# Moving the size pass of expert 1's first matrix into the attention's tail, its rows ahead of two raw pieces, and the later raw pieces and all converted pieces onto GpSimd's queue

## The chip, the cores and the metric

One core of a Trainium2 chip runs the whole program. Its engines, as the profile names them: PE (matmul; PEld is its weight load), DVE, ACT, POOL, and SP, which computes nothing and issues DMAs. A row "SPq" or "POOLq" is an issue of a DMA by that engine. The metric is the device time of one execution in microseconds; the median of three runs is compared.

## The reference, cut to what matters

Three layers in a row. First an attention with a decay (softmax-free), 4 batches of 576 tokens, 8 heads of 64. Then a mixture of 8 experts: each token goes to one expert `e`, found by a gate and a running rule along the sequence, and becomes `p[e] * (max(x @ w1[e], 0) @ w2[e])` with `w1[e]` 512x1024 and `w2[e]` 1024x512. Last a Fourier mixing with a layer norm and a two-matrix channel block whose weights `w_ch1` and `w_ch2` are 64-bit floats in the input.

```python
h = np.maximum(x[b, s] @ w1[e], 0.0)
out[b, s] = p[e] * (h @ w2[e])
...
ch = np.maximum(un @ w_ch1, 0.0) @ w_ch2
```

The kernel reads `w_ch1` and `w_ch2` as pairs of 32-bit integers and builds 32-bit floats from them.

## The kernel before, in words

**Order of the work.** `attention` runs 18 steps and routes tokens into rows of `xs` in DRAM, sorted by expert. Its tail (the calls after the loop, lines 760 to 800) already computes the hidden layer of the 256 tokens of expert 0's second part (`hidden`, line 692). Then `moe` runs: two output tiles of that part (line 1111), then the loop over experts `e = 0..7` (line 1119). Expert `e` has eight hidden blocks `f` (12 matmuls each of `n` columns: weights high times tokens high, low times high, high times low), then one output tile per 128 tokens (24 matmuls of 512 columns each). `n` is 128 for expert 0 in this loop and 416 for the first of the sorted experts, which the text calls expert 1; 320 or 288 for the next ones.

**Preparing a matrix.** A matrix comes as four pieces of 128x1024 floats (512 KB each, `Weights.load`, issued by SP, tile `wst`). Each needs its size: an ACT pass of absolute values with a running sum (`absmax`, line 234), which writes its useless output into the target `wh`. From the four sums DVE makes a small diagonal (`peak`, line 243, last operation line 255), PE spreads it over the partitions (`spread`, line 260), DVE makes the scale (`scale`, lines 266 and 269), and each piece is then split (`split`): ACT writes the high half (line 276), DVE the low half (line 281).

**A hidden block's exit.** `relu` (line 816): ACT writes the high half (823), DVE the low half (825). Hidden blocks rotate through four PSUM banks, so block 4 of an expert waits until DVE has read block 0.

**Converting.** 14 jobs (`Doubles`) turn a raw 1 MB piece of `w_ch1` or `w_ch2` into a 512 KB piece in DRAM (`ch`), in the shadow of the experts. A job is `load` (SP, tile `raw`, two buffers), `first` (DVE, lines 294, 296, 298), `second` (DVE, lines 303, 306), `absmax` (ACT, tile `ab`) and `store` (SP, line 338). `halves` (line 924) lists by hand at which block or tile each of these and each step of the next matrices is issued.

**Tokens.** `fetch(e)` (line 1005) reads the rows of expert `e` by a transposing DMA into `xt` (line 1012) and then their metadata `mt` with one to five small DMAs (lines 1025, 1028). `pad(e)` (line 1040) writes zeros into `xs` ahead; a later `fetch` waits for it.

**Every queue runs in order.** An engine's instruction that waits holds back all behind it. SP issues all of the loads above, so a raw load that waits for its buffer holds back the next weights and tokens. All SP transfers are on one hardware queue; the indirect stores of POOL (line 851) are on another, made by software. Line 402 puts the scratch row of the routing into expert 1's low half (`spare[1]`), so `beyond` (line 2063), its last reader, must come before the first split.

Of the kernel before, what the change touches and what calls it, by code (L numbers as in the profile page):

```python
# [9 lines left out]
FP32 = mybir.dt.float32  # L10
# [10 lines left out]
E, FF = 8, 2048  # L21
# [17 lines left out]
CAP = max(CAPS)  # L39
# [170 lines left out]
class Weights:  # L210
# [9 lines left out]
    def load(self, j):  # L220
        t = self.pool.tile([128, 1024], FP32, tag="wst", name="wst")
        src = self.src[j]
        to = t.rearrange("p (a d) -> p a d", a=2) if len(src.shape) == 3 else t
        self.nc.sync.dma_start(out=to, in_=src)
        self.pieces[j] = t
# [85 lines left out]
class Doubles:  # L311
# [4 lines left out]
        self.nc, self.pool, self.jobs, self.raw, self.t = nc, pool, jobs, {}, {}  # L316

    def load(self, j):
        r = self.pool.tile([128, 1024, 2], I32, tag="raw", name="raw", bufs=2)
        src = self.jobs[j][0]  # L320
        to = r.rearrange("p (a d) c -> p a d c", a=2) if len(src.shape) == 4 else r
        self.nc.sync.dma_start(out=to, in_=src)
        self.raw[j] = r

    def first(self, j):
# [9 lines left out]
        w.size(i, self.t[j].bitcast(FP32), x)  # L335

    def store(self, j):
        self.nc.sync.dma_start(out=self.jobs[j][1], in_=self.t[j].bitcast(FP32))


def attention(keep, tc, nc, A, xs, rows, hook, beside, after, zeros, first, spare, hid0, mt0):

    ctx = ExitStack()
    cp = ctx.enter_context(tc.tile_pool(name="const", bufs=1))
# [57 lines left out]

    carry = keep.tile([128, 17], BF16, name="carry")
    V.memset(carry, 0.0)
    room = spare[1][0:1, 0, :].bitcast(FP32)
    n_i, pick, tally, who, low, start, beyond = order(nc, A, keep, room, carry, onesb)
    slot_i = const("slot_i", [128, N], I32)
    slot_f = const("slot_f", [128, N])
# [381 lines left out]
    next(early[4])  # L790
    first.low(6)
    first.low(7)
    next(early[5])
    next(early[6])
    next(early[7])
# [4 lines left out]
    return idn, n_i, who, low, start, beyond  # L800


def products(nc, ps, h, l, xt, f):

    for i, (m, x) in enumerate(((h, 0), (l, 0), (h, 4))):
        for k in range(4):
            nc.tensor.matmul(  # L807
                out=ps,
                lhsT=m[:, k, 128 * f : 128 * f + 128],
                rhs=xt[:, x + k, :],  # L810
                start=(k == 0 and i == 0),
                stop=(k == 3 and i == 2),
            )


# [48 lines left out]
class Late:  # L864


    def __init__(self, nc, w, pool, x2, rows):
        self.nc, self.w, self.pool, self.x2, self.rows = nc, w, pool, x2, rows
        self.n, self.hid = CAPS[E - 1] - HEAD, None

    def hidden(self, fs, bank):

# [104 lines left out]
def moe(octx, tc, nc, A, xs, x2, rows_in, rows_out, pieces, weights, who, conv, low, start, beyond, z, hid0, mt0, wst, small):  # L977
# [6 lines left out]
    p2 = pool(name="p2", bufs=3, space=PSUM)  # L984
    weights(0).shared.bank = lambda: p2.tile([128, 512], FP32, tag="ps2", name="peak")[:, 0:128]
    X = {}
    end = Late(nc, weights(E - 1), wst, x2, rows_out)

    side = {}
    for k in (2, 4):  # L990
# [14 lines left out]
    def fetch(e):  # L1005
        n = CAPS[e] if e < E - 1 else HEAD
        xt = wk.tile([128, 8, n], FP16, tag="xt", name="xt", padded_shape=[128, 8, CAP])
        at = lambda a, m: slice(OFF + a, OFF + a + m) if e == 0 else bass.ds(low(e) + a, m)
        for j in range(2) if e == 0 else (None,):

            a, b = (0, 2) if j is None else (j, j + 1)
            i = nc.sync.dma_start_transpose(out=xt[:, 4 * a : 4 * b, :], in_=xs[at(0, n), 512 * a : 512 * b])
            if e == 0:
                rows_in.before(i)
            apart(e, i)
        if e == E - 1:
# [12 lines left out]
        if e == E - 1:  # L1029
            k = (n + 127) // 128  # L1030
            i = nc.sync.dma_start(
                out=mt[:, k : k + m // 128, :], in_=meta(n, m // 128 * 128).rearrange("(t p) c -> p t c", p=128)
            )
            apart(e, i)
            more = m % 128
            for j in range(0, 128, more) if more else ():
                apart(e, nc.sync.dma_start(out=mt[j : j + more, k + m // 128, :], in_=meta(n + m // 128 * 128, more)))
        X[e] = (xt, mt)

    def pad(e):  # L1040
        m = CAPS[e] - ZERO
        i = nc.sync.dma_start(
            out=xs[bass.ds(start(e), m), :].bitcast(I32).rearrange("(t p) c -> p t c", p=32),
            in_=z[0:32].bitcast(I32).unsqueeze(1).to_broadcast([32, m // 32, XW // 2]),
        )
        apart(e, i)

    def factors(w, mt, tiles):

        q = wk if w is not end.w else small  # L1050
        fs = q.tile([128, 5], FP32, tag="fs", name="fs", bufs=3)

        def fill():
            nc.vector.tensor_tensor(out=fs[:, 4:5], in0=w.inv[:, 0:1], in1=w.inv[:, 1:2], op=ALU.mult)
            nc.vector.tensor_scalar(
                out=fs[:, 0:tiles], in0=mt[:, 0:tiles, 1].bitcast(FP32), scalar1=fs[:, 4:5], scalar2=None, op0=ALU.mult
            )

        return fs, fill
# [15 lines left out]
        w1.load(p)  # L1075
    fetch(0)
    pad(1)
    conv.load(0)
    conv.load(1)
    fetch(1)  # L1080

    def begin():
        for p in range(4):
            w1.absmax(p)
        w1.peak(0)

    def parts():
        beyond()
        w1.spread(0)
        w1.scale(0)  # L1090
        w1.split(0)
        w1.split(1)

    def convert(n):
        conv.first(n)
        conv.second(n)
        conv.store(n)
        conv.load(n + 2)

    def sizes():  # L1100
        for p in range(4, 8):
            w1.absmax(p)
        convert(0)
        w1.peak(1)
        conv.absmax(0)
        convert(1)

    fs, fill = factors(weights(0), mt0, 2)
    fill()
    for t in range(2):  # L1110
        out(weights(0), hid0, mt0, fs, t, n, [(begin, parts)[t]])

    v = weights(2)
    first = [[] for _ in range(8)]
    for f, p in ((1, 2), (3, 3)):
        first[f].append(partial(w1.split, p))
    for f, p in zip((2, 3, 4, 5), range(4)):
        first[f].append(partial(v.load, p))
    for e in range(E):
        w, n = weights(e), CAPS[e] if e < E - 1 else HEAD  # L1120
        if e == E - 1:
            pieces.more = None
        xt, mt = X.pop(e)
        tiles = (n + 127) // 128

        todo = halves(weights, conv, 2 * e, 8, [("fetch", (fetch, e + 1))] if e + 1 < E else ()) if e else first
        hid = wk.tile([128, 2, 8, n], FP16, tag="hid", name="hid", padded_shape=[128, 2, 8, CAP])
        hid = [hid[:, x] for x in range(2)]
        for f in range(8):
            ps = p1.tile([128, CAP], FP32, tag="ps1", name="ps1")[:, 0:n]  # L1130
            products(nc, ps, *w.dst, xt, f)
            for do in todo[f]:
                do()
            if f == 4 and e + 2 < E:
                pad(e + 2)
            for _ in relu(nc, ps, hid, f):
                pass
        fs, fill = factors(w, mt, tiles + (end.n + 127) // 128 if e == E - 1 else tiles)
        if e == E - 1:
            end.fs = fs  # L1140

        def sides(mt=mt, tiles=tiles, n=n, e=e):
            for i, m in ((n // 128, n % 128), (tiles + end.n // 128, end.n % 128 if e == E - 1 else 0)):
                if m:

                    to, k = mt[:, i, 0:1], 128 // m
                    nc.vector.tensor_scalar(out=to, in0=to, scalar1=float(k), scalar2=side[k], op0=ALU.mult, op1=ALU.add)

        late = 0 < e < E - 1
        if not late:  # L1150
# [998 lines left out]
def fused_kernel(tc, A, out, stop=None):  # L2149
    nc = tc.nc  # L2150
    with ExitStack() as ctx:
# [5 lines left out]
        with tc.manual_schedule():  # L2157
# [101 lines left out]
                for p in range(4):  # L2259
                    weights(1, who).load(p)  # L2260

            idn, n_i, who, low, start, beyond = attention(keep, tc, nc, A, xs, rows_in, hook, beside, after, z, weights(0), bufs[1], hid0, mt0)
            fill.close()
            tp = ctx.enter_context(tc.tile_pool(name="tp", bufs=1, reuse_waits="tile"))
            tables = []
# [62 lines left out]
```

## Time and profile before

| | us |
|---|---|
| median of 3 runs | 802.59 (800.28 to 808.28) |
| the profiled execution | 806.81, its span 805.0 |
| PE busy in the span | 738.7 (92%) |
| DVE, ACT, POOL busy | 591.2, 411.8, 130.0 |

The rows below come from the profiled execution. Times in a timeline are counted from the span's start. The expert stage runs from about 130 to 349 us; the Fourier and channel stage follows. A busy PE is not a PE at its peak, and matmul ends are modelled. PEclk is the granted clock of PE as a share of 2.4 GHz; 0.5 is its other level, 1.2 GHz.

### The profile page before, as it was taken

The numbers are of one execution on the slowest core, as the hardware profiler recorded it, in microseconds if no ns is written. First come the engines' busy times: TensorE is split into PE (matmuls) and PEld (weight loads), VectorE is DVE, ScalarE is ACT, GpSimd is POOL, SyncE is SP. The second block draws the span as 40 slices with busy tenths as digits, with TensorE's granted clock in tenths as the row PEclk, the third lists the DMA queues.
The fourth block names the chain that finished last, engine by engine and source line by source line (L and its number), as shares of the span: only waits on it lengthen the run. The fifth ranks groups of instructions, "written<-read, shape, count | busy, mean of one in ns | idle before, by whom it ended". The sixth has DMA issues, their size and how long they took to land. (4 is left out here: it accounts for less than half of the span.)

```text
span 805.0 us, 17230 instructions
## 1 busy us (share of the span) xinstructions
PE 738.7 (92%) x6571; PEld 552.4 (69%) x6571; DVE 591.2 (73%) x1432; ACT 411.8 (51%) x829; POOL 130.0 (16%) x225
## 2 busy tenths in 40 slices
PE   7889898898999998889989998979899999999996
PEld 5778774644666555557634546868788888888885
DVE  3577886887889887957697986968968495737362
ACT  1355655676978797844836534515523361404140
POOL 3555443103012201113000011010010101010101
PEclk9999999999999999999999999999999999999998
DMA  8997439999999998961447357620370016210000
GB/s 288 354 295 270 163 107 275 244 330 339 289 379 281 270 362 292 265 217 42 130 130 273 132 173 193 181 66 2 104 207 2 27 53 171 53 39 16 27 2 27
DMA packets 91930, 142.29 MB, mean 177 GB/s; under 512 B 48116, under 2 KB 49017, under 8 KB 90814
## 3 DMA queue, kind: packets, MB, share of 16 engines
q1 hardware_dynamic: 87246, 126.78, 50.7%
q0 software_dynamic: 4592, 14.31, 4.7%
q8 instruction: 54, 0.88, 0.5%
q14 instruction: 38, 0.31, 0.1%
HBM read 97.55 MB, written 35.12 MB: 165 GB/s over the span
## 5 line engine op out<-in xcount | busy, mean ns | idle before, releaser
L1628 PE MATMUL g<-gxt,wh 128*128 128x256 f16 (+1 forms) x992 | 142.9, 284 | 4.6 <-DMA gxt<-un 3.4
L1942 PEld LDWEIGHTS <-hd 128*128 128x128 f16 x1176 | 115.1, 98 | 28.0 <-issue 7.7
L1628 PEld LDWEIGHTS <-wh 128*128 128x128 f16 x1056 | 103.0, 98 | 30.0 <-issue 8.3
L281 DVE SCALAR_TENSOR_TENSOR wl<-wst,ws,wh 128x1024 f16<-128x1024 f32 (+1 forms) x82 | 100.6, 1252 | 11.3 <-ACT wh L276 11.1
L276 ACT ACTIVATE wh<-wst,ws 128x1024 f16<-128x1024 f32 x80 | 89.4, 1141 | 28.7 <-DVE ws L269 28.3
L807 PE MATMUL ps<-xt,wh 128*128 128x320 f16 (+4 forms) x544 | 80.0, 285 | 12.1 <-DMA xt<-xs 7.5
L837 PE MATMUL ps<-wh,hid 128*128 128x512 f16 (+2 forms) x528 | 84.6, 302 | 0.2 <-ACT hid L823 0.2
L807 PEld LDWEIGHTS <-wh 128*128 128x128 f16 x640 | 58.6, 101 | 37.5 <-issue 16.0
L1942 PE MATMUL g<-wh,hd 128*128 128x256 f16 x448 | 79.9, 276 | 4.2 <-DVE u L1971 2.0
L1802 POOL DMA_INDIRECT out<-u,orow x18 | 19.3, 1075 | 392.0 <-DVE u L1971 293.6
L1628 PE MATMUL g<-gxt,wl 128*128 128x256 f16 (+1 forms) x496 | 79.5, 283 | 0.0
L837 PEld LDWEIGHTS <-hid 128*128 128x128 f16 (+2 forms) x792 | 46.5, 100 | 44.4 <-issue 4.7
L1913 DVE SCALAR_TENSOR_TENSOR s<-g,r 128x256 f32<-128x256 f32 x168 | 53.2, 372 | 30.6 <-ACT hd L1907 29.9
L234 ACT ACTIVATE wh<-wst 128x1024 bf16<-128x1024 f32 x66 | 69.3, 1051 | 3.8 <-DVE wst L306 3.8
L1971 DVE SCALAR_TENSOR_TENSOR u<-g,ffs,u 128x256 f32<-128x256 f32 (+1 forms) x63 | 34.2, 568 | 50.4 <-PE g L1942 48.5
L1906 ACT ACTIVATE r<-g 128x256 f32<-128x256 f32 x56 | 21.1, 377 | 91.7 <-PE g L1628 85.7
L1886 ACT ACTIVATE hd<-s 128x640 f16<-128x640 f32 x56 | 41.3, 737 | 47.1 <-DVE s L1913 47.1
L1942 PE MATMUL g<-e,hd 128*128 128x256 f16 x504 | 60.0, 273 | 5.5 <-DVE u L1971 4.5
L851 POOL DMA_INDIRECT x<-y,mt x25 | 32.3, 1291 | 197.5 <-ACT y L849 143.6
L1942 PE MATMUL g<-wl,hd 128*128 128x256 f16 x224 | 61.8, 276 | 0.0
L1628 PEld LDWEIGHTS <-wl 128*128 128x128 f16 x528 | 51.7, 98 | 11.4 <-issue 0.5
L837 PE MATMUL ps<-wl,hid 128*128 128x512 f16 (+2 forms) x264 | 56.5, 301 | 0.1
(302 smaller groups left out, 1301.0 us busy)
## 6 DMA issues: line engine op xcount, KB each, us to landing
wst<-in_moe_w SPq DMA_DIRECT2D x64, 512.0 KB
raw<-in_ch SPq DMA_DIRECT2D x14, 1024.0 KB
qk<-in_qkv SPq DMA_DIRECT2D x18, 512.0 KB
vk<-in_qkv SPq DMA_DIRECT2D x16, 512.0 KB
pair<-ch SPq DMA_DIRECT2D x32, 256.0 KB
ch<-d SPq DMA_DIRECT2D x14, 512.0 KB
wst<-ch SPq DMA_DIRECT2D x14, 512.0 KB
u<-u SPq DMA_DIRECT2D x9, 512.0 KB
```

The source lines that it names most:

```text
L234: self.nc.scalar.activation(out=x, in_=t, func=ACTF.Abs, accum_out=self.am[:, j : j + 1])
L276: self.nc.scalar.activation(out=self.dst[0][:, j, :], in_=self.pieces[j], func=ACTF.Copy, scale=self.by(j))
L281: self.nc.vector.scalar_tensor_tensor(out=l[:, j, c], in0=self.pieces[j][:, c], scalar=self.by(j), in1=h[:, j, c], op0=ALU.mult, op1=ALU.s ...
L807: nc.tensor.matmul(out=ps, lhsT=m[:, k, 128 * f : 128 * f + 128], rhs=xt[:, x + k, :], start=(k == 0 and i == 0), stop=(k == 3 and i == 2),)
L837: nc.tensor.matmul(out=ps[r * j : r * j + r, 0:d], lhsT=hid[x][:, f, 128 * t : 128 * t + r], rhs=m[:, 4 + f // 2, c : c + d], start=(f == ...
L851: nc.gpsimd.indirect_dma_start(out=x2[:, :].rearrange("t (k d) -> (t k) d", k=k), out_offset=bass.IndirectOffsetOnAxis(ap=mt, axis=0), in_ ...
L1628: nc.tensor.matmul(out=ps, lhsT=m[:, k + 4 * (f // 8), 128 * (f % 8) : 128 * (f % 8) + 128], rhs=xt[x][:, k, :], start=(k == 0 and i == 0) ...
L1886: nc.scalar.activation(out=hd[:, 0, 2:7], in_=s, func=ACTF.Copy, scale=C2 / 2)
L1906: nc.scalar.activation(out=r, in_=p[:, 1:3], func=ACTF.Relu)
L1913: V.scalar_tensor_tensor(out=d, in0=x, scalar=0.0, in1=y, op0=ALU.max, op1=op)
L1942: nc.tensor.matmul(out=ps, lhsT=hid[k][:, y, x, :], rhs=E[w][m][k], start=(k == 0 and m == y == 0), stop=(k == 7 and y == 1),)
L1971: V.scalar_tensor_tensor(out=y, in0=p, scalar=fs[:, c : c + 1], in1=y, op0=ALU.mult, op1=ALU.add)
```

## The change: what it does

Expert 1's first matrix: its four size passes leave `begin` and go into the attention's tail, ahead of the exits of hidden blocks 6 and 7 of expert 0's second part. Its spread stands inside the second output tile and no longer behind it, and all four splits follow at once. The scratch row moves to the high half of piece 6, so `beyond` moves from ahead of the scale to hidden block 7 of expert 0. The size passes of pieces 4 and 5 of expert 1 move up to block 0 of expert 0.

Expert 0's eight blocks are computed in two groups of four banks: all high-times-high products of a group, then high-times-low, then low-times-high.

SP's queue: `fetch(1)` now stands ahead of raw pieces 0 and 1. Raw pieces 2 to 13 and all 14 stores are issued by POOL. In `sizes`, `peak(1)` of expert 1 stands between `first(0)` and `second(0)`, not behind both.

```diff
     def load(self, j):
+        q = self.nc.gpsimd if j > 1 else self.nc.sync
...
-        self.nc.sync.dma_start(out=to, in_=src)
+        q.dma_start(out=to, in_=src)
...
     def store(self, j):
-        self.nc.sync.dma_start(out=self.jobs[j][1], in_=self.t[j].bitcast(FP32))
+        self.nc.gpsimd.dma_start(out=self.jobs[j][1], in_=self.t[j].bitcast(FP32))
...
-    room = spare[1][0:1, 0, :].bitcast(FP32)
+    room = spare[0][0:1, 6, :].bitcast(FP32)
...
     first.low(7)
+    sizes()
     next(early[5])
...
     fetch(0)
     pad(1)
+    fetch(1)
     conv.load(0)
     conv.load(1)
-    fetch(1)
...
     def parts():
-        beyond()
-        w1.spread(0)
         w1.scale(0)
-        w1.split(0)
-        w1.split(1)
+        for p in range(4):
+            w1.split(p)
...
     def sizes():
-        for p in range(4, 8):
-            w1.absmax(p)
-        convert(0)
+        for p in range(6, 8):
+            w1.absmax(p)
+        conv.first(0)
         w1.peak(1)
+        conv.second(0)
+        conv.store(0)
+        conv.load(2)
         conv.absmax(0)
-        convert(1)
+        conv.first(1)
+        conv.second(1)
+        conv.store(1)
+        conv.load(3)
...
-    for f, p in ((1, 2), (3, 3)):
-        first[f].append(partial(w1.split, p))
+    for p in range(4, 6):
+        first[0].append(partial(w1.absmax, p))
+    first[7].append(beyond)
...
+            if e == 0 and f % 4 == 0:
+                four = [bank()[:, 0:n] for _ in range(4)]
+                for part in (0, 2, 1):
+                    for g in range(4):
+                        products(nc, four[g], *w.dst, xt, f + g, (part,))
...
+            def sizes():
+                for p in range(4):
+                    weights(1).absmax(p)
```

**SP's queue around the tokens of expert 1.** Before, from the pad (`xs<-z`) on; `xt` are the tokens, `mt` their metadata, TENSOR_LOAD reads the row number into SP:

```order
L1042 DMA xs<-z 32x9x528
L322 DMA raw<-in_ch 128x2048 x2
L2046 TENSOR_LOAD n_i
L2046 ISA x2
L1012 ISA
L1012 DMA_TRANSPOSE xt<-xs 128x8x416
L1025 ISA
L1025 DMA mt<-xs 128x3x2
```

Now, at the same place, to the first weight piece of the matrix after expert 1's:

```order
L1050 DMA xs<-z 32x9x528
L2056 TENSOR_LOAD n_i
L2056 ISA x2
L1020 ISA
L1020 DMA_TRANSPOSE xt<-xs 128x8x416
L1033 ISA
L1033 DMA mt<-xs 128x3x2
...
L1036 DMA mt<-xs 32x2
L323 DMA raw<-in_ch 128x2048 x2
```

The two raw loads moved behind the transposing load and five metadata loads.

**DVE at the start of the conversion, just behind expert 0's hidden blocks.** Before (`d` is the converted piece, `wm` and `diag` are `peak(1)` of expert 1):

```order
L1055 TENSOR_SCALAR fs<-mt,fs 128x1
L294 TENSOR_SCALAR d<-raw 128x1024
L296 TENSOR_SCALAR d<-d 128x1024
L298 TENSOR_SCALAR d<-d 128x1024
L303 SCALAR_TENSOR_TENSOR d<-raw,d 128x1024
L306 SCALAR_TENSOR_TENSOR d<-raw,d 128x1024
L250 TENSOR_REDUCE wm<-am 128x1
L251 TENSOR_SCALAR wm<-wm 128x1
L255 TENSOR_SCALAR diag<-idn,wm 128x128
```

Now:

```order
L1062 TENSOR_SCALAR fs<-mt,fs 128x1
L294 TENSOR_SCALAR d<-raw 128x1024
L296 TENSOR_SCALAR d<-d 128x1024
L298 TENSOR_SCALAR d<-d 128x1024
L250 TENSOR_REDUCE wm<-am 128x1
L251 TENSOR_SCALAR wm<-wm 128x1
L255 TENSOR_SCALAR diag<-idn,wm 128x128
L303 SCALAR_TENSOR_TENSOR d<-raw,d 128x1024
L306 SCALAR_TENSOR_TENSOR d<-raw,d 128x1024
```

The diagonal stands two long operations earlier, still behind the first operation that needs raw piece 0; behind these rows follow, in both, the whole of job 1 and then the spread's reduction.

**POOL's queue from the two stores of expert 0's second part on.** Before, the indirect stores (`y` into `x2`) stand alone:

```order
L851 DMA x_58<-y,mt_88 2304x512
L186 MEMSET mark_x_74 1x8
L851 DMA x_58<-y,mt 2304x512
L186 MEMSET mark_x_74 1x8
```

Now:

```order
L855 DMA x_58<-y,mt_88 2304x512
L186 MEMSET mark_x_74 1x8
L339 DMA ch<-d 128x1024
L323 DMA raw<-in_ch 128x2048
L339 DMA ch<-d 128x1024
L323 DMA raw<-in_ch 128x2048
L855 DMA x_58<-y,mt 2304x512
L186 MEMSET mark_x_74 1x8
L339 DMA ch<-d 128x1024
L323 DMA raw<-in_ch 128x2048
```

Each store and each raw load from piece 2 on now stands among the indirect stores, behind the conversion that it waits for.

## Rows read from the trace of the kernel before

**Rows 1.** Stages: us, busy PE, PEld, DVE, ACT, POOL (instructions), clock, DMA share, GB/s

```profile
141.30:145.10 3.80, 3.80 (x40) 3.76 (x39) 3.52 (x5) 2.76 (x6) 1.57 (x2) 0.55 1.05 377
...
153.90:156.20 2.30, 0.06 (x2) 0.04 (x1) 2.19 (x6) 1.73 (x3) 0.00 (x0) 1.00 0.75 23
...
196.70:301.80 105.10, 102.01 (x808) 64.11 (x812) 93.02 (x157) 89.62 (x151) 15.06 (x20) 1.00 1.00 321
...
304.90:309.00 4.10, 4.10 (x21) 2.74 (x21) 2.33 (x8) 0.73 (x1) 1.34 (x3) 0.58 0.77 188
```

**Rows 2.** Waits of PE, 115 to 165 us: us in total, times, longest

```profile
PE ps L807 <- DMA xt<-xs: 4.7, 2, 2.4
```

**Rows 3.** Timeline around expert 1: start, us, engine, line, operation [idle before <- releaser]

```profile
139.35 2.95 SPq L322 DMA_DIRECT2D raw<-in_ch  x2
...
144.49 7.63 SPq L1012 DMA_TRANSPOSE xt<-xs  x1
...
149.68 0.69 DVE L294 TENSOR_SCALAR d<-raw 128x1024 int32<-128x1024 int32 x1
...
152.40 0.42 SPq L1025 DMA_DIRECT2D mt<-xs  x1
...
153.09 2.72 SPq L1028 DMA_DIRECT2D mt<-xs  x4
...
154.65 0.29 DVE L255 TENSOR_SCALAR diag<-idn,wm 128x128 bf16<-128x128 f32 x1
...
156.16 0.86 PE L807 MATMUL ps<-xt,wh 128*128 128x416 f16 x4 [2.24 <-DMA xt<-xs]
...
156.97 1.23 SPq L224 DMA_DIRECT2D wst<-in_moe_w  x3
...
158.29 1.22 DVE L306 SCALAR_TENSOR_TENSOR d<-raw,d 128x1024 int32<-128x1024 int32 x1
...
163.03 0.58 DVE L825 SCALAR_TENSOR_TENSOR hid<-ps,hid 128x416 f16<-128x416 f32 x1
...
171.25 0.69 DVE L294 TENSOR_SCALAR d<-raw 128x1024 int32<-128x1024 int32 x1 [2.03 <-DMA raw<-in_ch]
...
173.09 0.59 PE L837 MATMUL ps<-wh,hid 128*128 128x512 f16 x2
```

**Rows 4.** Waits of SP, 130 to 200 us

```profile
SPq L1012 <- DMA xs<-z: 1.1, 1, 1.1
```

**Rows 5.** Timeline of an earlier transposing load, in the attention's tail

```profile
109.55 2.69 SPq L680 DMA_TRANSPOSE wh<-xs  x2
...
113.41 0.61 PE L807 MATMUL ps<-wh,wh 128*128 128x256 f16 x4 [0.78 <-DMA wh<-xs]
```

**Rows 6.** Timeline, later waits of PE and DVE in the expert stage

```profile
177.42 0.22 PE L260 MATMUL ps<-diag,onesb 128*128 128x128 bf16 x1 [1.57 <-DVE diag L255]
...
184.09 1.67 SPq L322 DMA_DIRECT2D raw<-in_ch  x1
...
193.85 0.72 DVE L294 TENSOR_SCALAR d<-raw 128x1024 int32<-128x1024 int32 x1 [5.22 <-DMA raw<-in_ch]
...
196.71 0.23 PE L260 MATMUL peak<-diag,onesb 128*128 128x128 bf16 x1 [2.17 <-DVE diag L255]
...
304.89 0.65 PE L807 MATMUL ps<-xt,wh 128*128 128x288 f16 x4 [2.84 <-DMA xt<-xs]
```

**Rows 7.** Timeline of ACT in the attention's tail

```profile
129.93 0.38 ACT L821 ACTIVATE r<-ps 128x256 f32<-128x256 f32 x1 [4.59 <-DVE wl L281]
...
132.25 1.04 ACT L234 ACTIVATE wh<-wst 128x1024 bf16<-128x1024 f32 x1
```

**Rows 8.** POOL's mark (ns: least, median, most) and DVE beside its longest

```profile
L186 POOL MEMSET mark_x<- x25: 94/94/646, 138.3 to 380.6; 1x8 f32 x25
...
222.79 0.69 DVE L298 TENSOR_SCALAR d<-d 128x1024 int32<-128x1024 int32 x1
...
222.87 0.65 POOL L186 MEMSET mark_x<- 1x8 f32 x1
```

More of the change, by code (lines that the diff above doesn't have):

```diff
@@ L337, in store, with attention @@
     def store(self, j):
-        self.nc.sync.dma_start(out=self.jobs[j][1], in_=self.t[j].bitcast(FP32))
-def attention(keep, tc, nc, A, xs, rows, hook, beside, after, zeros, first, spare, hid0, mt0):
+        self.nc.gpsimd.dma_start(out=self.jobs[j][1], in_=self.t[j].bitcast(FP32))
+def attention(keep, tc, nc, A, xs, rows, hook, beside, after, sizes, zeros, first, spare, hid0, mt0):
     ctx = ExitStack()
@@ L800, in attention, with products @@
     return idn, n_i, who, low, start, beyond
-def products(nc, ps, h, l, xt, f):
-    for i, (m, x) in enumerate(((h, 0), (l, 0), (h, 4))):
+def products(nc, ps, h, l, xt, f, parts=range(3)):
+    last = 2 if len(parts) == 3 else 1
+    for i in parts:
+        m, x = ((h, 0), (l, 0), (h, 4))[i]
         for k in range(4):
@@ L811, in products @@
                 start=(k == 0 and i == 0),
-                stop=(k == 3 and i == 2),
+                stop=(k == 3 and i == last),
             )
@@ L867, in __init__, with w @@
     def __init__(self, nc, w, pool, x2, rows):
-        self.nc, self.w, self.pool, self.x2, self.rows = nc, w, pool, x2, rows
+        self.nc, self.of, self.pool, self.x2, self.rows = nc, w, pool, x2, rows
         self.n, self.hid = CAPS[E - 1] - HEAD, None
+    @property
+    def w(self):
+        return self.of()
     def hidden(self, fs, bank):
@@ L986, in moe @@
     X = {}
-    end = Late(nc, weights(E - 1), wst, x2, rows_out)
+    end = Late(nc, lambda: weights(E - 1), wst, x2, rows_out)
     side = {}
@@ L1046, in pad, with factors @@
         apart(e, i)
-    def factors(w, mt, tiles):
-        q = wk if w is not end.w else small
+    def factors(w, mt, tiles, q=wk):
         fs = q.tile([128, 5], FP32, tag="fs", name="fs", bufs=3)
@@ L1077, in moe, with parts @@
     pad(1)
+    fetch(1)
     conv.load(0)
     conv.load(1)
-    fetch(1)
-    def begin():
+    def parts():
+        w1.scale(0)
         for p in range(4):
+            w1.split(p)
+    def sizes():
+        for p in range(6, 8):
             w1.absmax(p)
-        w1.peak(0)
-    def parts():
-        beyond()
-        w1.spread(0)
-        w1.scale(0)
-        w1.split(0)
-        w1.split(1)
[L1094 to L1100, printed above, removed]
-        for p in range(4, 8):
-            w1.absmax(p)
-        convert(0)
+        conv.first(0)
         w1.peak(1)
+        conv.second(0)
+        conv.store(0)
+        conv.load(2)
         conv.absmax(0)
-        convert(1)
+        conv.first(1)
+        conv.second(1)
+        conv.store(1)
+        conv.load(3)
     fs, fill = factors(weights(0), mt0, 2)
     fill()
+    w1.peak(0)
     for t in range(2):
-        out(weights(0), hid0, mt0, fs, t, n, [(begin, parts)[t]])
+        out(weights(0), hid0, mt0, fs, t, n, (parts,) if t else (), partial(w1.spread, 0) if t else None)
     v = weights(2)
     first = [[] for _ in range(8)]
-    for f, p in ((1, 2), (3, 3)):
-        first[f].append(partial(w1.split, p))
+    for p in range(4, 6):
+        first[0].append(partial(w1.absmax, p))
+    first[7].append(beyond)
     for f, p in zip((2, 3, 4, 5), range(4)):
@@ L1129, in moe @@
         for f in range(8):
-            ps = p1.tile([128, CAP], FP32, tag="ps1", name="ps1")[:, 0:n]
-            products(nc, ps, *w.dst, xt, f)
+            if e == 0 and f % 4 == 0:
[3 more added lines that the diff above has]
+                        products(nc, four[g], *w.dst, xt, f + g, (part,))
+            if e == 0:
+                ps = four[f % 4]
+            else:
+                ps = bank()[:, 0:n]
+                products(nc, ps, *w.dst, xt, f)
             for do in todo[f]:
@@ L1137, in moe @@
                 pass
-        fs, fill = factors(w, mt, tiles + (end.n + 127) // 128 if e == E - 1 else tiles)
+        fs, fill = factors(w, mt, tiles + (end.n + 127) // 128, small) if e == E - 1 else factors(w, mt, tiles)
         if e == E - 1:
@@ L2260, in after, with sizes @@
                     weights(1, who).load(p)
-            idn, n_i, who, low, start, beyond = attention(keep, tc, nc, A, xs, rows_in, hook, beside, after, z, weights(0), bufs[1], hid0, mt0)
+            def sizes():
+                for p in range(4):
+                    weights(1).absmax(p)
+            idn, n_i, who, low, start, beyond = attention(keep, tc, nc, A, xs, rows_in, hook, beside, after, sizes, z, weights(0), bufs[1], hid0, mt0)
             fill.close()
```

## The prediction

> **What bounds the kernel now.** I read the stages first. In the expert stage PE is the engine that is full: from 196.7 to 301.8 us it is busy 102.01 of 105.10 us [rows 1]. So a change in this stage is worth only what it adds to or takes from the few gaps of PE, and I went on to the waits of PE and then to the timeline at each gap. Near expert 1 there are two gaps, both for tokens (`xt`): 4.7 us in total [rows 2], of which the second, 2.24 us, ends at 156.16 [rows 3]. Later there are 1.57 and 2.17 us in front of a spread, whose diagonal DVE makes late, and 2.84 us for the tokens of a later expert [rows 6]. DVE made those diagonals late because it stood in front of a raw piece: 2.03 us [rows 3] and 5.22 us [rows 6]. All gaps that this change can reach are thus 2.24 + 1.57 + 2.17 + 2.84 = 8.8 us, and what the clock adds: behind the last one the granted clock is 0.58 over 4.1 us [rows 1], the lower level for most of it, which costs 4.1 x 0.42 = 1.7 us. After the first gap it is 0.55 for 3.8 us [rows 1]; that gap stays, since `fetch(0)` and what is ahead of it in SP's queue are unchanged.
>
> **The tail of the attention.** Four size passes of 1.04 us [rows 7] move from behind ACT's last hidden exit to before the last two. ACT stands idle there for 4.59 us [rows 7], but the last pieces may land late in that gap; two exits then end up to 0.8 us later, and PE reads them in the eighth block of the tile that runs. I take 0.3 us. Bounds: 0 and the four passes, 4.2 us. Regrouping expert 0's 96 matmuls removes and adds none; it needs four banks at once, so block 4's group waits for four exits; I take 0, at most the 1 us that four exits might lag. Moving `beyond` costs DVE nothing: it stood in the way of the scale and now stands where DVE has no other work. All of this lies ahead of the new wait below and is swallowed by it, up to 3.7 us.
>
> **Tokens of expert 1 and raw pieces 0 and 1.** Before, two raw loads (2 MB) were issued at 139.35, ahead of the transposing load at 144.49 [rows 3]. That load cannot start much earlier: SP waited 1.1 us for the pad to land right before it [rows 4], and the pad stays where it is. But nothing large is ahead of it any more. An earlier transposing load of 256 rows took SP 2.69 us [rows 5]; 416 rows are 4.4 us, so SP is through at 148.9 and not at 152.1, and with the 1.2 us from the end of such an issue to PE's start [112.24 to 113.41, rows 5] the tokens are there at 150.1. PE is done with expert 0 at 156.16 - 2.24 = 153.9, with the tail's 0.3 at 154.2: the gap of 2.24 us goes.
>
> What is late next is raw piece 0. SP needs 3.7 us for the five metadata loads (from 152.12 to 155.81, rows 3) and so issues it at 148.9 + 3.7 = 152.6. It lands 0.4 us of issue (1.23 for three, rows 3) + 2.8 us of transfer (1.05 MB at 377 GB/s, rows 1) + 1.2 us later: at 157.0. The lower bound leaves out the last term, 155.8; the upper is the 9.8 us which the loaded queue took from the issue at 184.09 to the start at 193.85 [rows 6], 162.4. I take 157.0, since the DMAs moved only 23 GB/s at that place [rows 1]. DVE began this conversion at 149.68 [rows 3], so DVE is 7.3 us late.
>
> What is queued behind that wait: on DVE the diagonal, both conversions, then the scale and the exit of hidden block 0. From 149.68 to the diagonal's end at 154.94 less the two second operations (2.46 us) is 2.8 us in the new order, so PE's spread, queued behind block 0 (one block is (173.09 - 156.16) / 8 = 2.12 us, rows 3), gets it at 157.0 + 2.8 + 0.2 = 160.0: PE stands from 156.3, 3.7 us. Then PE does blocks 1 to 3, and block 4 waits for block 0's exit. Before, the conversions ended at 159.51, 9.83 us after their start, and the exit 4.1 us later at 163.61 [rows 3], 1.0 us ahead of PE's block 4 at 156.16 + 4 x 2.12 = 164.6. Now the exit ends at 157.0 + 9.83 + 4.1 = 170.9 and block 4 starts at 171.0: **PE is 6.4 us behind the old kernel**, the 2.24 us gained already counted.
>
> **Later raw pieces on POOL's queue.** Before, raw pieces 2 and 4 were asked for by SP late, behind other loads; now POOL asks as soon as DVE is through with the buffer. Raw 2 is asked for about 162.5 and needed at 171.25 - 2.03 + 7.3 = 176.5; even 9.8 us suffice. So the 2.03 us go, DVE is 5.3 us late, and the spread at 177.42 comes at 182.7, where PE (6.4 behind, but formerly waiting 1.57 us) arrives at 182.3: 5.3 us behind. Raw 4 likewise: DVE asks 5.22 us earlier, and the 2.17 us go: 3.1 us behind. I price POOL's issues themselves at nothing: POOL is busy 15.06 of 105.10 us [rows 1], its indirect stores have three output buffers, and each raw piece has a spare of over 5 us; without that cover the price is the slow rival below.
>
> POOL's mark takes 94 ns and once 646 ns, beside a DVE operation of the kind that starts each conversion [rows 8]. The Trainium skill (SBUF — State Buffer, section SBUF: two separate sides) says that while DVE runs an operation that uses both ports GpSimd is locked out and cannot write the descriptors of its own DMAs. The trace agrees for a memset; no run here shows a plain DMA on this queue. By that rule the three such operations of a conversion delay a raw load by up to 3 x 0.69 = 2.1 us, which changes the sum by nothing while the spare holds, and feeds the slow rival.
>
> The gap of 2.84 us and its clock, together 4.5 us: the tokens of that expert stood in SP's queue behind a raw piece and a store, 1.57 MB or 4.9 us at 321 GB/s [rows 1]. These now go on another queue but over the same DMA engines. Bounds 0 and 4.5 gained; nothing in the trace decides, I take 2.2. Two new waits of some 4 us may bring the low clock once more, 0 to 1.7 us (the second of them partly behind DVE's lateness); I take 0.6.
>
> **Sum:** 6.4 - 1.1 - 2.2 - 2.2 + 0.6 = +1.5 us. The profiled execution took 806.81 (span 805.0), so 808.3 by its own time; it is 4.2 us above the median of the three runs, 802.59, and by that the forecast is 804.
>
> **Rivals.** (a) *Slow: the conversions do not catch up.* If raw 2 lands after 178.5 and raw 4 later than 199, because POOL's issues are held by DVE, the waits of 2.03 and 5.22 us stay: PE keeps DVE's 7.3 us, the later gap stays, and with 1.2 us of clock it is +8.5 us, 811. For it: the 646 ns row and DVE's load of 93.02 of 105.10 us [rows 1]; against it: the spares. (b) *Fast: raw piece 0 in time.* If it lands by 148.8, block 4 finds its exit done, and the gaps go without the price: -(1.9 + 1.57 + 2.17 + 4.5) = -10.1 us, 792.5. Against it: SP itself is not free before 148.9. A landing between costs 1 us per us, and so does a later one, up to +5.4 us at 162.4. (c) *The other queue only shares the engines.* Then the gap at 304.89 stays whole: +3.7 us, 806.3. The Trainium skill (DMA: Bandwidth & Descriptors, section Queues, rings and completion order) says that each DMA engine serves its queues in turn, packet by packet. No row here shows two large transfers on two queues; by that rule the 1.57 MB still pass before the tokens, which is this rival. (d) The whole gap goes: -0.7 us, 801.9.
>
> **Chances.** A measurement of this kernel can tell about 1% (8 us) from no change. Forecast with (d) 0.55, its own range 799 to 807; (c) 0.20; (a) 0.15; (b), or a landing early enough for most of it, 0.10. Faster by over 1% needs (b): 0.10. Slower needs (a): 0.15. Within 1%: 0.75. The range takes in (a) at its edge and half the way to (b): 797 to 811.
>
> **What would show it.** Right: no wait for tokens at expert 1's start; DVE idle in front of L294 from about 150 to 157; PE idle some 3.7 us before the first spread of expert 1 and again before its block 4; no DVE wait for raw pieces after that. Wrong: raw piece 0's conversion starting before 153, or no gap at the spread (then the sum is too high by that); DVE waits for raw pieces from POOL's queue (then too low); a different length of what follows the expert stage, which I leave as it is.

## The result, and the profile after

| | before | after |
|---|---|---|
| median, executions | 803.05 us (6: 800.28 to 808.28) | 813.16 us (6: 810.96 to 829.71) |
| ratio | | 1.0129 [1.0092, 1.0166] |
| profiled execution, its span | 806.81, 805.0 | 812.88, 811.0 |

The change makes the kernel 1.3% slower; the forecast was 804 us, at most 811. The ratio leaves out executions over 1.5% above a kernel's fastest, so it is not the quotient of the medians. The executions after are also spread far more widely than those before, which is half of the story below. The profiled execution before lies 3.8 us above its median, the one after at its median, so the two traces differ by 6.1 us and the medians by 10.1.

Expert 1 went much as forecast. PE's waits after, 115 to 165 us, which answer to [rows 2]:

```profile
PE peak L260 <- DVE diag L255: 4.4, 1, 4.4
PE ps L811 <- DVE hid L829: 3.0, 1, 3.0
```

The timeline after, which answers to [rows 3] (the code below line 320 has moved down, in these rows by one to eight lines: L1020 is the former L1012, L811 the former L807, L829 the former L825):

```profile
142.78 3.92 SPq L1020 DMA_TRANSPOSE xt<-xs  x1
...
144.12 1.95 PE L811 MATMUL ps<-xt,wh 128*128 128x128 f16 x32 [3.00 <-DVE hid L829]
...
150.41 0.84 SPq L323 DMA_DIRECT2D raw<-in_ch  x2
...
155.84 0.70 DVE L294 TENSOR_SCALAR d<-raw 128x1024 int32<-128x1024 int32 x1 [6.30 <-DMA raw<-in_ch]
...
158.62 0.26 PE L260 MATMUL peak<-diag,onesb 128*128 128x128 bf16 x1 [4.37 <-DVE diag L255]
...
169.73 1.35 PE L811 MATMUL ps<-xt,wh 128*128 128x416 f16 x4 [2.36 <-DVE hid L829]
```

The tokens' waits are gone; DVE stands 6.30 us for raw piece 0, PE 4.37 us at the spread and 2.36 us at block 4. The conversion's start is 155.84 - 149.68 = 6.2 us late.

Both programs have the same 6571 matmuls, in the same order but for expert 0's regrouped ones and a few neighbours that changed places, so their starts can be paired by position. After minus before, worked out from the two traces:

| matmul at (before) | 156.16, expert 1 | 164.65, block 4 | 169.40, after a stretch at the low clock | 177.42 | 196.71 | 304.89 | 320.97 | 349.10 | 796.95, the last | end of span |
|---|---|---|---|---|---|---|---|---|---|---|
| PE later by, us | -4.2 | +5.1 | +6.8 | +5.0 | +1.9 | -0.5 | +4.8 | +5.4 | +3.5 | +5.9 |

So PE starts expert 1 early, is 6.8 us behind within it, and has won that back by 304 us, nearly as the sum said. Then it loses 5 us within 20 us. The timeline after at that place; its first line answers to the last of [rows 6]:

```profile
304.43 0.65 PE L811 MATMUL ps<-xt,wh 128*128 128x288 f16 x4 [0.50 <-DMA xt<-xs]
...
306.65 0.76 POOL L323 DMA_DIRECT2D raw<-in_ch  x1
...
307.41 0.60 POOL L339 DMA_DIRECT2D ch<-d  x1
307.67 7.68 SPq L224 DMA_DIRECT2D wst<-in_moe_w  x8
...
314.91 1.06 ACT L234 ACTIVATE wh<-wst 128x1024 bf16<-128x1024 f32 x1 [2.25 <-DMA wst<-in_moe_w]
...
318.87 1.06 ACT L234 ACTIVATE wh<-wst 128x1024 bf16<-128x1024 f32 x1 [1.48 <-DMA wst<-in_moe_w]
...
320.86 0.65 PE L811 MATMUL ps<-xt,wh 128*128 128x288 f16 x4 [2.33 <-DVE hid L829]
```

The tokens' gap fell from 2.84 to 0.50 us. But ACT's size passes now wait for weight pieces, and since they stand ahead of the hidden exits in ACT's queue, PE waits for an exit. The weights are issued while POOL's raw piece and store are under way.

A last piece of the loss lies behind all of PE's work: at the last matmul PE is 3.5 us late, at the end of the span 5.9. The last row of an engine that computes, before (span 805.0) and after (span 811.0):

```profile
799.00 0.10 POOL L186 MEMSET mark_out<- 1x8 f32 x1
...
802.49 0.09 POOL L186 MEMSET mark_out<- 1x8 f32 x1
```

From its end to the end of the span are 5.9 us before and 8.4 after. In the traces POOL is then in the closing instruction of its queue, a DRAIN, of 6.38 us before and 8.51 us after.

### The profile page after: what moved, and what is told of

It is laid out like the page before. It is cut to its first block, busy times and chain, and to the rows that moved or that the text cites. A ratio compares the mean times of both kernels' runs of the same rounds, so it can differ in the third digit from the quotient of the medians.

```text
span 811.0 us, 17234 instructions
## 1 busy us (share of the span) xinstructions
PE 738.9 (91%) x6571; PEld 550.0 (68%) x6571; DVE 593.2 (73%) x1432; ACT 411.9 (51%) x829; POOL 142.8 (18%) x251
## 5 line engine op out<-in xcount | busy, mean ns | idle before, releaser
L811 PE MATMUL ps<-xt,wh 128*128 128x320 f16 (+4 forms) x544 | 80.4, 286 | 13.8 <-DVE hid L829 10.2
L811 PEld LDWEIGHTS <-wh 128*128 128x128 f16 x640 | 57.6, 101 | 47.7 <-issue 30.3
```

Of the source, the lines that this page charges most:

```text
L811: nc.tensor.matmul(out=ps, lhsT=m[:, k, 128 * f : 128 * f + 128], rhs=xt[:, x + k, :], start=(k == 0 and i == 0), stop=(k == 3 and i == last),
```

## The experiments

**Which edit (e1 to e4).** Two parts are undone, one by one and both. e1 has all transfers on SP:

```diff
-        q = self.nc.gpsimd if j > 1 else self.nc.sync
+        q = self.nc.sync
-        self.nc.gpsimd.dma_start(out=self.jobs[j][1], in_=self.t[j].bitcast(FP32))
+        self.nc.sync.dma_start(out=self.jobs[j][1], in_=self.t[j].bitcast(FP32))
```

e2 has the old order of SP's loads, e3 has both of these; e4 is the kernel before with the two lines on POOL's queue alone.

```diff
-    fetch(1)
     conv.load(0)
     conv.load(1)
+    fetch(1)
```

> The changed kernel with every raw load and every store issued by SP again, nothing else undone. Theory S (weights share the DMA engines with POOL's transfers, and the late weights hold ACT and with it the hidden exits of expert 6): ACT waits for no weight piece near 310 to 325 us, the 4.3 us of PE waits for hidden exits and the 2 us around them there go; but the raw waits of DVE (2.0 and 5.2 us) come back and so the price of the late raw piece 0 is not earned back: about 808 us. Rival L (the late raw piece 0 alone makes the loss): POOL's queue does no harm, so the time stays at 813 us or gets worse by the returning raw waits, up to 817.

> The changed kernel with raw pieces 0 and 1 issued ahead of the tokens of expert 1 again, nothing else undone. Theory S: DVE finds raw piece 0, the 4.4 and 2.4 to 3.0 us of PE waits in expert 1 go, a wait for tokens of 2 to 4 us comes back in front of expert 1, and the loss near expert 6 of 5 us stays: 808 to 810 us. Rival L: the loss is gone, 800 to 803 us.

> Both edits at once: raw pieces 0 and 1 ahead of the tokens, all raw loads and stores on SP; left of the change are the size passes in the tail, the regrouping of expert 0's products and the moved routing end. Theory S and rival L: neither loss is there; by the tail's earlier splits expert 1 may start 0 to 2 us earlier: 801 to 804 us. If it stays over 808, the cause lies in the tail or the regrouping, and both theories fall.

> The kernel before with only the queue moved: raw pieces 2 to 13 and all stores on POOL. Theory S: the raw waits of DVE (2.0 and 5.2 us) and with them 1.6 and 2.2 us of PE waits go, the token wait near 305 us goes (2.8 us and 1.7 us of clock), and the new loss of 5 us near expert 6 comes: 799 to 801 us. Rival L: no such loss, 793 to 796 us.

| kernel | tokens of expert 1 | POOL's queue | median us (range) | ratio to before |
|---|---|---|---|---|
| changed | ahead of raw 0, 1 | all | 813.16 (810.96 to 829.71) | 1.0129 [1.0092, 1.0166] |
| e1 | ahead | none | 805.66 (803.37 to 808.35) | 1.0021 [0.9998, 1.0044] |
| e2 | behind | all | 806.97 (801.64 to 810.33) | 1.0011 [0.9980, 1.0042] |
| e3 | behind | none | 803.33 (800.45 to 806.71) | 0.9991 [0.9963, 1.0019] |
| e4 | behind, rest as before | all | 805.77 (803.57 to 808.92) | 1.0027 [1.0002, 1.0053] |

By the ratios neither edit costs more than 0.3% alone (at most 0.5% by their intervals); together they cost 1.3%. The rest of the change (e3) shows no gain or loss. So neither theory stands by itself: what costs is that the two edits meet. Both theories missed e4, which they had under 801 us. In their profiles e2 and e4 are 7.3 and 6.4 us ahead of the kernel before at its 304.89, so POOL's queue does gain there; by 320.97 e2 has lost all of it (PE waits 5.3 us for hidden exits, ACT 6.3 us for weights) and e4 2.8 us, and both pay 2.4 us at the end of the program (last paragraph of this section). e1's waits of PE at expert 1 are those of the changed kernel (4.4 us at the spread, 5.4 for hidden exits up to 180 us), and yet it ends near the kernel before; the raw waits that its forecast had come back did not, DVE waits there for raw piece 0 alone (6.3 us).

**The weights of the last stretch (e5, e6).** e5 takes only the last transfers off POOL's queue:

```diff
-        q = self.nc.gpsimd if j > 1 else self.nc.sync
+        q = self.nc.gpsimd if 1 < j < 13 else self.nc.sync
-        self.nc.gpsimd.dma_start(out=self.jobs[j][1], in_=self.t[j].bitcast(FP32))
+        (self.nc.gpsimd if j < 11 else self.nc.sync).dma_start(out=self.jobs[j][1], in_=self.t[j].bitcast(FP32))
```

e6 is the reverse, with `j > 12` and `j > 10` in these two lines.

> The changed kernel with its last raw piece (13) and the last three stores (11, 12, 13) back on SP's queue, all others left on GpSimd's. Theory S (these transfers, issued at 306 to 312 us by GpSimd, take the DMA engines from the eight weight pieces that SP issues at 307.7): ScalarE's waits for wst by 296 to 326 us fall from 5.1 us to under 1.5, TensorE's for hid there from 3.6 to under 1, the lead of about 0.5 us at 304 is kept, and the time falls from 813 to 807 to 809 us. Theory L (the late first piece sets it all, and the queue does nothing): 812 to 814 us, waits at 315 to 321 us as they were.

> The reverse: all raw pieces and stores on SP as in e1, but raw piece 13 and stores 11, 12 and 13 on GpSimd's queue. S: the waits for wst and hid at 310 to 322 us come back (3 us or more of TensorE's for hid), and the time goes from e1's 805.7 to 809 to 811 us. L: 805 to 807 us. If all of the transfers on the other queue matter and not the last ones, then also 805 to 807 us, while e5 stays near 811.

e5: 812.55 us (805.41 to 835.76), ratio 1.0078 [1.0037, 1.0119]. Of its 12 executions six took 805 to 809 us, three 816 to 820 and three 829 to 836. In its profile ACT's waits for weights at 296 to 326 us are gone, as expected, and PE's for hidden exits are 0.3 us; that execution took 808.37 us, but the median did not follow. e6: 805.50 us (800.43 to 809.17), ratio 1.0033 [1.0006, 1.0060]; ACT waits 1.0 us for weights and PE does not wait. The last weights are a real wait of some executions, but they do not make the long ones, and e6 is a miss of theory S. Yet the six short executions of e5 lie where S put them (807 to 809 us) or just under it.

**Raw piece 0, and the first try at a better kernel (e7, e8).** e8 is e2 with e5's edit. e7:

```diff
-    fetch(1)
     conv.load(0)
+    fetch(1)
     conv.load(1)
```

> The changed kernel with raw piece 0 issued ahead of the second tokens' load and raw piece 1 behind it. If the late piece 0 alone makes the stall at expert 1, the 4.4 us wait at the spread and the two low-clock stretches at 156 and 170 us go, as in e2, and the time is 805 to 809 us. If piece 1 counts as much, TensorE's wait for hid at block 4 stays and the time is 809 to 812 us.

> Both mended: raw pieces 0 and 1 ahead of the second tokens, and raw piece 13 and stores 11 to 13 on SP; the rest on GpSimd's queue. S and the stall at expert 1 as two separate costs: TensorE is 6 to 7 us ahead of the kernel before at 304 us, as in e2, and keeps most of it past 330 us; 798 to 802 us, the fastest so far. If the lead is lost elsewhere in the expert stage or behind it, 803 to 806 us.

e7: 809.64 us (804.94 to 836.49), ratio 1.0066 [1.0030, 1.0101]. The spread's wait went, but PE waits 9.1 us in two times for hidden exits, so piece 1 counts too; five of its 12 executions are over 816 us. e8: 802.24 us (797.00 to 813.91), ratio 0.9975 [0.9953, 0.9998]; expected were 798 to 802.

**What makes the long executions (e9 to e15).** None of e1 to e4 and e6 is over 810.4 us, while e5 and e7 have six and five of 12 over 816. e9 is the changed kernel with the second of e1's two edits alone (all stores on SP), e10 with the first alone (all raw pieces on SP). e11 to e13 are the changed kernel itself, e14 is e5's and e15 e7's once more.

> The changed kernel with all stores back on SP's queue; raw pieces from 2 on stay on GpSimd's. Up to here e5 and e7 had executions of 805 to 810 us and others of 816 to 836 us, the changed kernel 811 to 830, and e1, e3 and e6, with nearly all of these transfers on SP, none over 810. If the stores make the long executions (theory: GpSimd stands at a store until the conversion is done, and the next raw piece and the rows' scatters stand behind it), they go: 805 to 808 us, none over 811. If the raw pieces make them, a third to a half of the executions are over 815 us.

> The reverse: all raw pieces on SP's queue, the stores on GpSimd's. If the stores make the long executions, a third or more are over 815 us and the median is 809 to 813; if the raw pieces do, all lie within 802 to 810 us, as in e1.

> The changed kernel once more, one profiled execution: 811 to 813 us by what four of its six executions took, or 820 to 830 by the other two. In the latter case the added time shows as a wait for raw pieces, weights or tokens that the first profile does not have (theory T: a DMA transfer lands late), or as the same waits with more stretches at the low TensorE clock (rival C: clock alone, no transfer later by over 2 us).

e9: 807.22 us (805.30 to 811.51), 1.0054 [1.0020, 1.0089]. e10: 808.11 us (805.84 to 812.25), 1.0041 [1.0013, 1.0070]. Neither part alone makes them: a miss for both theories, it takes raw pieces and stores together. e11 took 805.58 us, outside both of its forecasts: the changed kernel has short executions as well.

> The changed kernel timed again on another chip, since its executions so far were 805.6 on one chip and 811 to 830 us on another. If its time is spread by what the transfers do in each execution (theory T), it again has some at 805 to 808, most at 811 to 814 and some over 815 us, and a median of 809 to 814. If the spread was the first chip's (rival H), all lie within 804 to 809 us and the ratio to the kernel before is 1.002 to 1.006.

> One more profiled execution of the changed kernel. T: at 811 us or more, ScalarE waits 3 us or more for weight pieces somewhere in experts 2 to 6, and TensorE then 2 us or more for hid; at 805 to 807 us it does not. H: 804 to 808 us.

> e5's kernel once more for its profile: 805 to 808 us by half of its executions, 816 to 836 by the other half. T: in the long case a transfer (raw piece, store, weight or the tokens) lands over 5 us later than in e5's profile, and an engine's wait for it is what grows. Rival C: no transfer is later by over 2 us, and only the stretches at the low clock grow.

> e7's kernel once more for its profile: 805 to 810 us by 7 of its 12 executions, 816 to 836 by five. As for e14, T says that a late transfer is the start of the loss, C that it is the clock alone.

e12, on a chip that neither e5 and e7 nor e11 ran on: 814.03 us (9 executions, 808.35 to 835.32), 1.0123 [1.0080, 1.0166]. So the spread is the kernel's and not one chip's. e13 is a long one, 830.82 us, and shows where it is lost. PE's waits in e13, 180 to 300 us:

```profile
PE ps L811 <- DMA xt<-xs: 21.5, 1, 21.5
```

One long wait, for the tokens of expert 3. The timeline of e13 up to it:

```profile
194.11 0.57 POOL L323 DMA_DIRECT2D raw<-in_ch  x1 [0.58 <-DVE d L306]
194.21 33.02 SPq L1020 DMA_TRANSPOSE xt<-xs  x1
...
203.10 0.58 POOL L323 DMA_DIRECT2D raw<-in_ch  x1 [3.03 <-DVE d L306]
203.67 0.57 POOL L339 DMA_DIRECT2D ch<-d  x1
...
245.83 1.23 PE L811 MATMUL ps<-xt,wh 128*128 128x320 f16 x4 [21.55 <-DMA xt<-xs]
```

The issue of the transposing load lasts 33 us; the kernel before took 10.51 us for the same one. Raw pieces 5 and 6 and stores 3 and 4 are issued within it; by the packets, raw 5 and store 3 are all but through before the load's first packet at 206.3 us, and raw 6 and store 4 run beside the load, later raw 7 too. What the DMAs did in e13 (windows; the last two columns are DMA share and GB/s, the third from last is the clock):

```profile
210.00:225.00 15.00, 14.29 (x106) 7.95 (x104) 12.00 (x22) 12.89 (x23) 2.27 (x3) 1.00 1.00 92
225.00:240.00 15.00, 0.00 (x0) 0.00 (x0) 0.00 (x0) 0.84 (x2) 2.76 (x6) 0.63 1.33 59
240.00:255.00 15.00, 9.17 (x56) 6.09 (x56) 8.15 (x14) 4.89 (x8) 1.27 (x2) 0.69 0.97 344
```

The DMA engines count as busy throughout (shares of 1.00 and 1.33) and move 59 to 92 GB/s, where they move 344 afterwards. The stores and raw pieces suffer in the same way: DVE stands 18.9 us for a store to leave its buffer, and POOL's next raw piece is held behind it. PE, idle for 21 us, is granted the lower clock for 20.5 us from 228.8 on. e14 (812.24 us) and e15 (811.01) are milder cases with waits of 4.5 and 5.5 us for the same tokens. So T holds, in that a late transfer starts the loss, and C falls. The transfer that e13's forecast named, the weights, was the wrong one: ACT waits at most 2.0 us for them there.

The DMA packets tell how long the transposing load ran (expert 3's tokens: first to last of its 2560 packets of 256 bytes; all packets of POOL's queue beside it; worked out from each trace):

| profiled kernel | raw 6 issued by POOL ahead of the load's first packet, us | load ran, us | MB of POOL's queue beside it | PE waited, us |
|---|---|---|---|---|
| before | (SP's queue) | 5.3 | 0 | 0 |
| e18 | (SP's queue) | 7.8 | 0 | 0 |
| e4 | 9.1 | 6.3 | 0.01 | 0 |
| e8 | 7.7 | 7.9 | 0.43 | 0 |
| e2 | 7.7 | 7.4 | 0.40 | 0 |
| e7 | 6.5 | 7.1 | 0.79 | 0 |
| e11, changed, 805.58 | 5.5 | 9.1 | 1.13 | 0 |
| e9, raw pieces only | 5.0 | 5.9 | 0.75 | 0 |
| changed, 812.88 | 4.9 | 10.7 | 1.31 | 0 |
| e5 | 3.9 | 12.2 | 1.57 | 0 |
| e15 | 3.7 | 21.7 | 1.64 | 5.5 |
| e12, changed, 814.03 | 3.6 | 16.6 | 1.62 | 0 |
| e14 | 3.3 | 20.6 | 1.67 | 4.5 |
| e13, changed, 830.82 | 3.2 | 37.0 | 2.44 | 21.5 |
| e17 (below) | 1.2 | 31.2 | 1.66 | 13.7 |

This is how the two edits meet. The late raw piece puts DVE behind, and POOL's raw 6 waits for DVE: it is issued at 202.25 us in the changed kernel and at 195.12 in e2. It then runs beside the tokens' load instead of ahead of it. Up to some 16 us the load hides behind PE's work on expert 2; what is beyond that PE waits. The bytes do not decide how long it takes: expert 2's tokens, in the same 812.88 us execution, loaded in 11.6 us beside 2.1 MB, where the kernel before took 3.9, and PE did not wait for them.

**The four transfers alone (e16 to e18).** e17 leaves only these four on POOL's queue:

```diff
-        q = self.nc.gpsimd if j > 1 else self.nc.sync
+        q = self.nc.gpsimd if 4 < j < 7 else self.nc.sync
-        self.nc.gpsimd.dma_start(out=self.jobs[j][1], in_=self.t[j].bitcast(FP32))
+        (self.nc.gpsimd if 2 < j < 5 else self.nc.sync).dma_start(out=self.jobs[j][1], in_=self.t[j].bitcast(FP32))
```

e16 takes them and all earlier ones off it (`j > 6` and `j > 4`). e18 is e2 with only the middle ones on it (`6 < j < 13` and `4 < j < 11`).

> The changed kernel with raw pieces 2 to 6 and stores 0 to 4 back on SP's queue, ahead of or behind the tokens' loads and never beside them; raw pieces 7 to 13 and stores 5 to 13 stay on GpSimd's. Theory X (the long executions are those in which raw pieces 5 and 6 and stores 3 and 4, issued by GpSimd at 193 to 203 us, run beside the transposing load of expert 3's tokens and hold it for 10 to 37 us instead of 4): the load of expert 3's tokens takes 4 to 7 us, no execution is over 813 us, the median is 806 to 809. Rival: any of GpSimd's transfers can do it, then a third of the executions are still over 815 us.

> The reverse: all on SP's queue as in e1, but raw pieces 5 and 6 and stores 3 and 4 on GpSimd's. X: the load of expert 3's tokens takes 10 us or more, and a third or more of the executions are over 812 us, against none of e1's over 809. Rival: 803 to 809 us, all of them, as in e1.

> What the runs so far would keep: raw pieces 0 and 1 ahead of the second tokens, as before the change, and GpSimd's queue only for raw pieces 7 to 12 and stores 5 to 10, which meet neither expert 3's tokens nor the last eight weight pieces; the rest of the change stays. 798 to 802 us and no execution over 808, if the lead that e2, e4 and e8 had at 304 us comes from these transfers; 802 to 804 us, as e3, if it came from the earlier ones.

e17: 821.22 us, all six executions between 818.06 and 825.66, ratio 1.0196 [1.0161, 1.0231], against 1.0021 for e1 with the four on SP. Its waits of PE, 180 to 300 us:

```profile
PE ps L811 <- DMA xt<-xs: 13.7, 1, 13.7
```

and its windows:

```profile
190.00:205.00 15.00, 14.85 (x176) 8.90 (x175) 11.05 (x18) 10.04 (x18) 5.91 (x10) 1.00 1.03 405
210.00:225.00 15.00, 14.71 (x109) 8.28 (x107) 12.42 (x22) 12.89 (x22) 1.87 (x3) 1.00 1.36 60
```

Raw 6 goes out 1.2 us ahead of the load's first packet, the load runs 31.2 us, and the rate falls from 405 to 60 GB/s. With the late raw piece, these four transfers are enough for a loss of that size and more. That does not make them the loss of every execution: in those of 812.88 and 814.03 us the load still hid. e16: 811.50 us (803.75 to 817.83), ratio 1.0052 [1.0018, 1.0086]. Expert 3's tokens now load in 4.8 us and nothing is over 818 us, but eight of 12 are over 809 and four over 813: half a miss. In its profile the load of expert 4's tokens runs 10.5 us beside 1.63 MB of POOL's next raw pieces and stores, and PE did not wait for it; PE loses some 6 us at 309 to 328 us, where ACT waits 6.5 us for weights. The rival, that any of POOL's transfers can do it, is right in so far as the time stays up; of the third over 815 us that it forecast, two of 12 came. e18: 804.58 us (800.79 to 808.58), ratio 0.9991 [0.9967, 1.0015]: nothing gained over e3. So the best is e8, 0.25% under the kernel before by an interval that all but reaches 1; its executions on that one chip are all there is for it.

**The end of the program (all runs).** From the start of the last matmul to the end of the span, in every profile, by how many of the 26 later raw loads and stores stand on POOL's queue:

| on POOL's queue | 0 | 4 | 12 | 14 | 16 | 22 | 26 |
|---|---|---|---|---|---|---|---|
| runs | before, e1, e3 | e6, e17 | e9, e18 | e10 | e16 | e5, e8, e14 | changed, e2, e4, e7, e11, e12, e13, e15 |
| us | 8.08 | 8.40 | 9.05 | 9.22 | 9.38 | 9.87 | 10.52 |

Runs with the same number agree within 0.01 us, whatever else they do and however long they take. Up to 22 each transfer adds 0.08 us, a raw load of 1 MB as much as a store of half of that (e9 has 12 loads, e18 six of each); all 26 add 2.4 us. Of these, 2.1 us are the longer DRAIN of POOL. Why it grows no run shows.

## Why the prediction was wrong

**Right: the path through expert 1.** Forecast and measured: raw 0 issued at 152.6 and 150.41, its conversion begun at 157.0 and 155.84, PE's stand at the spread 3.7 and 4.37 us, PE behind at block 4 by 6.4 and 5.1 us, and by 7.0 and 6.8 with the low clock that follows, no wait for raw pieces after that. Of this 5.5 us were to be won back up to 304 us and 7.2 were. So the sum had PE 1.5 us behind there and it was 0.5 us ahead: it held within 2 us. One gap went that I had said stays: the first wait for tokens, with its low clock; PE starts expert 0 in the loop 3.0 us earlier (138.27, before 141.29), and what brought these tokens forward was not looked for. Rivals (a) and (b) fell: DVE waits for no later raw piece in the first profile, and raw 0 was not in time.

**Right in the sum, wrong as a term.** Regrouping was priced at 0 to 1 us; PE stands 3.00 us at 144.12, where block 4's group waits for four exits. It was swallowed, since the changed kernel starts expert 1 4.2 us early, and e3, which keeps it, loses nothing to the kernel before.

**The step that failed: "I price POOL's issues themselves at nothing".** The issues are cheap (0.5 to 0.8 us each); the transfers behind them, and the queue's own end, are not. I asked what POOL's transfers do to the tokens at 304.89 alone, and priced them there by bytes, 1.57 MB at 321 GB/s, gained or not. That gap did go, 2.84 to 0.50 us. I did not ask the same of the other loads that POOL's transfers now run beside. Before, SP's single queue kept raw pieces, stores, weights and tokens apart in time; that order was lost. Two loads pay, and the end of the program pays too:

- Expert 3's tokens: 5.3 us before, 9 to 37 us after. Bytes over bandwidth do not give this: 1.3 to 2.4 MB are 4 to 7.5 us at 321 GB/s. The rate itself falls, to 59 GB/s in e13. In the profiled execution of 812.88 us and in e12's of 814.03 it still hid, so it is a loss of the long executions and not of these two; in e13 it cost 21.5 us and the clock. The lateness that I had counted as paid back by 304 us is what moves the four transfers there. Shown by e17 for these four; e2 and e4 show that the queue alone, without the lateness, costs 0.1 and 0.3%.
- The weights: ACT waits 5.1 us for them at 314 to 323 us, and through ACT's queue PE 3.6 us for hidden exits, the larger part of the +5.2 us between 304.9 and 321 in the profiled pair (the rest are spreads whose diagonal DVE made late). e12 has a like one at 293 (PE waits 3.3 us), e2 and e16 have it at 314 and 323 (5.0 and 3.2 us); e11, the short execution, has no such wait of PE. That POOL's transfers beside them cause it is read from the traces; e6 did not show it in the times, and e5 only in its short executions.
- The end: the prediction left "a different length of what follows the expert stage" as it is, that is at nothing. It measured +2.4 us in each profile with all 26 transfers on POOL's queue, 0.3% of the time, and is the one part of the loss that all profiles of the changed kernel show alike.

**The range.** Rival (c) had two queues share the DMA engines and a price of +3.7 us, but for one gap alone. No case of mine had a loss that differs from execution to execution; the before's executions gave no sign of that. The chance of 0.15 for slower was for a mechanism that did not occur: POOL's issues were not held, and no later raw piece was waited for.

**Open.** What makes the median. Of the 10 us, 2.4 are the end of the program; the rest of the usual 811 to 814 us, against the shortest of 805.58 and 808.35, is not isolated by any run. The profiles of 812.88 and 814.03 us hold waits for weights of 5.1 and 6.6 us and, behind them, PE's for hidden exits of 3.6 us each; the one of 805.58 us holds 2.5 us, and PE's are 0.3. Why e17, with fewer transfers on POOL's queue, is worse than the changed kernel was not tried. Nor was the cheapest mend, `peak(1)` ahead of `first(0)`, which takes the spread out from behind raw piece 0.

## What to carry to other kernels

One queue is also an order. Whoever moves transfers to a second queue should list, for each, what will be in flight beside it at its new time, transposing loads first, and price these pairs, not only the one load that was to come free. And a delay that is won back on the critical path is not gone if something off the path was moved by it: here 7 us of lateness on DVE, invisible at 304 us, decided which transfers met. Compare also what stands behind the last matmul: each transfer moved to POOL's queue was paid for once more there.

## What the runs showed of the hardware

- A transposing load of 655 KB (2560 packets of 256 bytes) ran 4 to 8 us with nothing of another queue beside it (e1 4.3, e18 7.8), and 9 to 37 us with 1.1 to 2.4 MB. The two together moved 59 to 92 GB/s in e13 and 60 in e17, the DMA engines busy all the while, against 344 and 405 shortly after or before. Single 8192-byte packets of POOL's queue are recorded with up to 8.7 us in e13, where their median is 0.31. The Trainium skill (DMA: Bandwidth & Descriptors, section Rules for kernel authors) says, in a row on corrupted data, that a transpose next to ordinary DMAs needs nothing; on corruption no run here bears, and for the time these traces disagree.
- With weights on the other queue, the packets of the profile go about one for one: at 290 to 297 us of the changed kernel some 65 packets of 4096 bytes of POOL's queue per us stand beside some 72 of 2048 bytes of SP's, so the weights got a third of the bytes. Here the rule of turns, packet by packet, that the prediction cited from the Trainium skill (DMA: Bandwidth & Descriptors, section Queues, rings and completion order) agrees, if a packet of the profile is one of that rule. Beside the transposing load the counts are far apart: at 229 to 238 us of e13, 650 packets of 256 bytes and 72 of 4096 or 8192.
- A plain transfer issued by POOL costs 0.08 us once more at the end of the program, in POOL's last DRAIN: 6.38 us with none, 8.51 us with 26, the same in every run within 0.01 us.
- Four profiled executions of the changed kernel took 805.58, 812.88, 814.03 and 830.82 us; of the longest, 21.5 us are one wait for tokens whose load met two transfers of the other queue.
